# Spectral mixing and S4D convolution on one core: the inverse's first step joined to the kernel taps in two quarters, the products of both halves in one instruction, other planning constants

## The chip, the cores and the metric

One core of one Trainium2 chip. The metric is the device time of one execution in microseconds (us). The kernel before the change takes 584.09 us (median of three runs, 583.81 to 584.11).

## What is computed

Two independent blocks share one program, and their outputs are concatenated. All data are float32.

```
# A: Fourier mixing, x is 2048 x 512
a = einsum("bsd,ed->bse", x, dft_hid_re);  b = einsum("bsd,ed->bse", x, dft_hid_im)
yA = einsum("ts,bse->bte", dft_seq_re, a) - einsum("ts,bse->bte", dft_seq_im, b)
# B: S4D, u is 2048 x 512, state size 128
K  = 2 * real(einsum("dn,dnl->dl", C * dt, exp(A * dt * l)))     # taps, 512 x 2048
yB = irfft(rfft(u, 4096) * rfft(K, 4096), 4096)[:2048] + u * D_skip
```

## The kernel before, in words

**The stream (A).** Both matrix products of A run as one long sequence of 128x128x512 matmuls, 1920 of them (line 366, `acc`). Each operand is split into a rounded part `hi` (ScalarE, line 221) and the rest `lo` (VectorE, line 225), and three matmuls make one product: hi·hi, lo·hi, hi·lo. A call of three is a *stream step*; there are 640. Raw operands arrive in tiles `raw` (7 of them, `RAWS`), are split into pairs of tiles (4 pairs, `DEPTH`); 28 operands go another way, with two GpSimd DMAs (lines 315 and 320).

**The convolution (B)** needs, in order: tables of powers on VectorE (products at line 605, sums at line 614; 16 chunks of 32 channels); for each chunk the *taps*, 64 small matmuls of tables (line 801, in the trace 128 matmuls and as many weight loads, since a float32 matmul appears twice); after two chunks the first DFT step of the taps (line 832); the same for u (line 890); then for each quarter of the channels (h = 0 to 3) and each of four blocks q a *product*: the second DFT step on TensorE (line 992), two ScalarE copies of its two halves out of PSUM (line 1006), on VectorE for each half the two elementwise multiplications (lines 1009 and 1011), then one subtraction (line 1019) and one addition (line 1022); then the *inverse's first step*, 16 small matmuls (line 1029, `f<-uk,ia`), whose result goes to DRAM; and when a quarter's four blocks are there, the *inverse's second step*, two calls of 16 matmuls (line 1078, `f<-zl,ib`).

**What sets the order.** Every engine works in program order, and that order comes from a planner in the kernel (class `Plan`): each piece of work is a generator that asks for an engine with a planned duration and an urgency; the planner always takes the request with the earliest planned start, in grains of `GRAIN` us, and among equals the lowest urgency number. The stream has urgency 5, so it fills TensorE wherever nothing else is ready; a call of another kind is put between stream steps at the moment when the planner thinks its data are there. Going from the stream to other matmuls and back has a planned price. `fetched` models the loading of the instructions. `LATE[h]` is the urgency of quarter h's product. A `Joined` piece can run its matmuls inside the next taps call instead of alone: the mechanism is there before the change, but with `JOIN = 0` no quarter uses it. The buffers `uk` and `z` exist once for quarters 0 to 2 (`b.n` is 1) and twice for quarter 3, so one product must have done its inverse's first step before the next may begin.

Of the kernel before, what the change touches and what calls it, by code (L numbers as in the profile page):

```python
# [11 lines left out]
AF = mybir.ActivationFunctionType  # L12
# [38 lines left out]
STREAM = 5  # L51
GRAIN = 0.05
BLOCK, ASKS, LASTS = 256, 110, 400
ASKED, APART_BY, COMES = 2.0, 3.8, 2.4
APART = None, True
LATE = 1, 1, 3, 1


def HELD():
    return 1  # L60


# [20 lines left out]
class Plan:  # L83
# [111 lines left out]
class Fnet:  # L195
# [149 lines left out]
    def matmuls(self):  # L345
        nc = self.nc
        for g in self.groups:
            still = (self.x, self.x_ev) if g[0] == "s" else (self.w, self.w_ev)
            items, acc = self.items[g], []
            for batch in [[i] for i in items[:-BATCH]] + [items[-BATCH:]]:  # L350
                for d in range(4):
# [3 lines left out]
                    for i in batch:  # L355
# [53 lines left out]
class Joined(Event):  # L409
# [5 lines left out]

    def run(self, got, shared=True):
        self.got, self.users = got, {k: 1 for k, _ in got}
        if shared:
            self.users[got[0][0]] = 2
        self.fn(got)  # L420

# [6 lines left out]
class Ssm:  # L428


    def __init__(self, tc, ctx, plan, fnet, nd, ldt, dsk, uG, f1u, f1k, w2, ia, ib, out):
# [14 lines left out]
        self.t1s, self.t2s, self.css = Sem(2), Sem(1), Sem(2)  # L446
        self.kss, self.res, self.xks = Sem(1), Sem(1), Sem(1)
        self.waiting, self.taps_left, self.pars = [], 16, Sem(1)
        self.sets, self.set_ev = {}, [Event(), Event()]
# [27 lines left out]
    def banks(self, n):  # L477
# [7 lines left out]
        self.plan.put(self.one)  # L485
        return got

    def give(self, k):
# [294 lines left out]
    def taps(self, ks, n, done):  # L783
# [4 lines left out]
        other = self.waiting.pop(0) if self.waiting else None  # L788
        got = yield from self.banks(2 if other else 1)
        k, p = got[0]  # L790
        yield "pe", 1.97 + (1.05 if other else 0), None, 320 if other else 256
        if other:
            other.run(got)
        t1, t2 = self.t1.pop(n), self.t2
# [13 lines left out]
        while self.waiting and not self.taps_left:  # L808
# [3 lines left out]
                             p[:, :, 256:].rearrange("p o (i l) -> p l o i", i=4), AF.Copy)  # L812
        if other:
            other.leave(k)
        else:
            self.give(k)
        done()

    def stage1_k(self, ks, n, ev):
# [6 lines left out]
        got = yield from self.banks(2)  # L826
        yield "pe", 1.11, None, 64
        for a in range(2):
# [50 lines left out]
    def stage1_u(self, k):  # L879
# [4 lines left out]
        got = yield from self.banks(2)  # L884
        yield "pe", 1.13, None, 32
        for r in range(2):
# [94 lines left out]
    def product(self, b, h, q, got, done):  # L981
# [22 lines left out]
        def half(r, k, p):  # L1004
            yield "act", act(1024), HELD
            a.activation(uk[:, r].rearrange("p g c n d -> p g (c n d)"), p, AF.Copy)  # L1006
            self.give(k)
            yield "dve", dve(512)
            v.tensor_tensor(P[:, r], t[:, r], u[:, r], op=OP.mult)  # L1009
            yield "dve", dve(512), *APART  # L1010
            v.tensor_tensor(t[:, r], t[:, r], u[:, r, :, ::-1], op=OP.mult)  # L1011
# [7 lines left out]
        v.tensor_tensor(u[:, :, :, 0], P[:, :, :, 0], P[:, :, :, 1], op=OP.subtract)  # L1019
# [3 lines left out]

        def run(got):
            for c, Y in enumerate((u, t)):
# [6 lines left out]
        if self.taps_left and h < JOIN:  # L1032
            self.waiting.append(w)
            yield w
        if w.got is None:
            got = yield from self.banks(2)
            yield "pe", 1.05, None, 64
            w.run(got, False)
        self.plan.put(b.uks)
# [27 lines left out]
    def inverse(self, b, h, i, n):  # L1067
# [4 lines left out]
        for o in range(0, n, 8):  # L1072
            nc.sync.dma_start(z[:, o:o + 8], self.zs[h].rearrange("s c l d -> (s c) l d")[:, n * i + o:n * i + o + 8])
        (k, ps), = yield from self.banks(1)
        yield "pe", 0.14 + 0.11 * n, None, 4 * n
        for w in range(n // 2):
            for y in range(2):
                nc.tensor.matmul(ps[64 * y:64 * y + 64, w // 4, PART * (w % 4):PART * (w % 4) + PART],  # L1078
                                 self.ib[:, n * i + 2 * w + y], z[:, 2 * w + y], start=True, stop=True,
                                 tile_position=(0, 64 * y))  # L1080
        o = n * i // 2
        for w in range(0, n // 2, 4):
            yield "act", act(512)
            nc.scalar.activation(z[:, w:w + 4], ps[:, w // 4].rearrange("p (w d) -> p w d", w=4), AF.Copy)
        self.give(k)
        yield "dma", load(32 * n, 270)
# [81 lines left out]
```

## Time and profile before

| what | value |
|---|---|
| median of three runs | 584.09 us |
| the profiled execution: its own time | 582.56 us |
| its span, first to last instruction | 580.8 us |
| TensorE busy | 571.1 us, 98% |
| VectorE busy | 512.5 us, 88% |
| ScalarE busy | 371.2 us, 64% |
| GpSimd busy | 40.3 us, 7% |
| granted TensorE clock, mean | 0.999 |

In the page, "PE" is TensorE's matmuls, "PEld" its weight loads, DVE VectorE, ACT ScalarE, POOL GpSimd. A matmul's row lasts longer than the distance to the next one, because matmuls overlap; a VectorE row overlaps the next one a little too. So distances from start to start are what add up, not durations. The span is divided into 40 slices of 14.5 us, with the busy share of each in tenths.

### The profile page before, as it was taken

What the parts mean: (1) busy time and instruction counts of PE and PEld (TensorE: products, weight loads), DVE (VectorE), ACT (ScalarE), POOL (GpSimd) and SP (SyncE); (2) the same over time, 40 slices, a digit from 0 to 9 for tenths busy, and PEclk for the clock granted to TensorE, in tenths of its full rate; (3) what the DMA queues carried; (4) which work ended last, traced back from release to release, by engine and by line L of the source; (5) the groups of instructions that cost most, each with busy time, mean ns of one, the idle gap of its engine ahead of it and who ended that gap; (6) DMA issues with size and microseconds to landing.
All of it is one profiled execution on the core that took longest, in us unless ns stands there. A gap on an engine that the chain in (4) does not pass through costs nothing.

```text
span 580.8 us, 15376 instructions
## 1 busy us (share of the span) xinstructions
PE 571.1 (98%) x6150; PEld 436.1 (75%) x6150; DVE 512.5 (88%) x911; ACT 371.2 (64%) x729; POOL 40.3 (7%) x60
## 2 busy tenths in 40 slices
PE   8999999999999999999999999999999999999996
PEld 6877777788777777778877777777687777776685
DVE  6999999999999999999999999999989999346410
ACT  4779665763777595768568585945588744445522
POOL 0000000000100000100000001001100000000000
PEclk9999999999999999999999999999999999999999
DMA  8999999986469767876797887479989995789564
GB/s 248 327 372 263 280 294 276 285 262 170 133 159 239 207 171 218 205 180 207 207 222 190 237 216 226 125 186 296 243 280 262 243 282 184 209 251 303 169 195 144
DMA packets 147831, 133.10 MB, mean 229 GB/s; under 512 B 47280, under 2 KB 107312, under 8 KB 147504
## 3 DMA queue, kind: packets, MB, share of 16 engines
q1 hardware_dynamic: 139408, 117.05, 66.7%
q0 software_dynamic: 8064, 14.68, 12.6%
q8 instruction: 48, 0.79, 0.6%
q10 hardware_dynamic: 288, 0.39, 0.2%
q14 instruction: 23, 0.19, 0.1%
HBM read 89.36 MB, written 42.73 MB: 227 GB/s over the span
## 4 chain that ended last, share of the span: by engine, by line
PE 70%; DVE 23%; issue 4%; DMA 2%; SPq 0%; ACT 0%; DVEq 0%; ACTq 0%
PE acc L366 55%; DVE prod L605 8%; DVE t L614 4%; PE f L992 4%; PE f L801 3%; DVE lo L225 3%; PE f L1029 3%; PE f L1078 2%; PE f L890 2%; DVE t L634 1%; PE f L832 1%; DVE z L1009 1%; DVE cs L675 1%; DMA zl<-zs 1%; DVE uk L1011 1%
## 5 line engine op out<-in xcount | busy, mean ns | idle before, releaser
L366 PE MATMUL acc<-hi,x_hi 128*128 128x512 f32 x640 | 258.2, 403 | 0.3 <-ACT hi L221 0.3
L366 PE MATMUL acc<-lo,x_hi 128*128 128x512 f32 x640 | 250.2, 391 | 0.0
L366 PE MATMUL acc<-hi,x_lo 128*128 128x512 f32 x640 | 249.7, 390 | 0.1
L605 DVE TENSOR_TENSOR prod<-t,cs 128x1024 f32<-128x1024 f32 (+4 forms) x192 | 163.1, 867 | 1.7 <-ACT t L723 0.6
L366 PEld LDWEIGHTS acc<-hi,x_hi 128*128 128x128 f32 x640 | 120.1, 188 | 49.8 <-issue 23.7
L366 PEld LDWEIGHTS acc<-hi,x_lo 128*128 128x128 f32 x640 | 120.3, 188 | 26.5 <-DVE x_lo L225 0.5
L366 PEld LDWEIGHTS acc<-lo,x_hi 128*128 128x128 f32 x640 | 120.3, 188 | 23.0 <-DVE lo L225 0.2
L221 ACT ACTIVATE hi<-raw 128x512 fp32r<-128x512 f32 x132 | 82.6, 627 | 64.0 <-PE acc L366 48.5
L225 DVE TENSOR_TENSOR lo<-raw,hi 128x512 fp32r<-128x512 f32 x132 | 90.1, 684 | 28.2 <-ACT hi L221 21.9
L614 DVE TENSOR_TENSOR t<-prod 128x512 f32<-128x512 f32 (+4 forms) x192 | 94.0, 511 | 1.0
L621 ACT ACTIVATE square<-t 128x256 f32<-128x256 f32 (+1 forms) x64 | 36.7, 573 | 31.0 <-DVE t L614 28.3
L320 POOL DMA_DIRECT2D lo<-in_sT x28 | 24.3, 868 | 214.1 <-ACT lo L318 33.8
L1006 ACT ACTIVATE uk<-f 128x1024 f32<-128x1024 f32 x32 | 31.1, 1017 | 11.8 <-PE f L992 11.8
L801 PEld LDWEIGHTS f<-t,t 128*32 128x32 f32 x2048 | 29.5, 110 | 7.9 <-issue 5.8
L801 PE MATMUL f<-t,t 128*32 128x64 f32 x2048 | 32.4, 220 | 1.9 <-issue 1.4
L389 ACT ACTIVATE y<-acc 128x512 f32<-128x512 f32 x47 | 28.0, 595 | 8.7 <-PE acc L366 8.6
L1009 DVE TENSOR_TENSOR z<-uk 128x512 f32<-128x512 f32 x32 | 21.9, 684 | 9.6 <-ACT uk L1006 7.4
L315 POOL DMA_DIRECT2D hi<-in_sT x28 | 16.2, 577 | 189.4 <-PE acc L366 147.0
L1044 ACT ACTIVATE z<-f 128x512 f32<-128x512 f32 x32 | 17.7, 592 | 13.3 <-PE f L1029 13.3
L634 DVE TENSOR_TENSOR t<-square 128x128 f32<-128x128 f32 (+1 forms) x64 | 24.6, 385 | 0.0
L992 PE MATMUL f<-xt,w 64*32 64x256 f32 x768 | 23.5, 379 | 0.0
L1011 DVE TENSOR_TENSOR uk<-uk 128x512 f32<-128x512 f32 x32 | 22.1, 690 | 0.9
(94 smaller groups left out, 490.7 us busy)
## 6 DMA issues: line engine op xcount, KB each, us to landing
raw<-in_sT SPq DMA_DIRECT2D x99, 256.0 KB, 5.4
p<-y SPq DMA_DIRECT2D x32, 256.0 KB, 3.2
xk<-xk_sb SPq DMA_DIRECT2D x32, 256.0 KB, 5.2
zs<-z SPq DMA_DIRECT2D x32, 256.0 KB, 3.3
zl<-zs SPq DMA_DIRECT2D x16, 512.0 KB, 5.0
raw<-p SPq DMA_DIRECT2D x32, 256.0 KB, 4.4
hi<-in_sT POOLq DMA_DIRECT2D x28, 256.0 KB, 4.6
lo<-in_sT POOLq DMA_DIRECT2D x28, 256.0 KB, 4.9
```

Of the source, the lines that this page charges most:

```text
L221: self.nc.scalar.activation(hi, src, AF.Copy)
L225: self.nc.vector.tensor_tensor(lo, src, hi.bitcast(F32), op=OP.subtract)
L366: nc.tensor.matmul(acc[d], l[:, cols], r, start=k == 0 and n == 0, stop=k == len(items) - 1 and n == 2)
L389: self.nc.scalar.activation(y, ps, AF.Copy, scale=-1.0 if g[2] == 1 else 1.0)
L605: self.nc.vector.tensor_tensor(p.rearrange("p k d c m -> p k (d c) m"), src.rearrange("p d c l -> p (d c) l")[:, None, :, rows].to_broadca ...
L614: self.nc.vector.tensor_tensor(dst[:, :, :, rows], p[:, 0], p[:, 1, :, ::-1], op=OP.add)
L621: self.nc.scalar.activation(sq, t[:, :, :, m // 2:m], AF.Square)
L634: self.nc.vector.tensor_tensor(t[:, :, 0, m:2 * m:2], box[0][:, :, 0], box[0][:, :, 1], op=OP.subtract)
L801: nc.tensor.matmul(ps[32 * j:32 * j + 32, i], t1[:, d, c], t2[:, d, c], start=c == 0, stop=c == 1, tile_position=(0, 32 * j))
L992: nc.tensor.matmul(got[r][1][32 * xx:32 * xx + 32, g, 256 * c:256 * c + 256], self.w2[rows, 2 * q + r, xx, 32 * c:32 * c + 32], xt[rows].r ...
L1006: a.activation(uk[:, r].rearrange("p g c n d -> p g (c n d)"), p, AF.Copy)
L1011: v.tensor_tensor(t[:, r], t[:, r], u[:, r, :, ::-1], op=OP.mult)
```

## The change

1. `JOIN` 0 becomes 2: in quarters 0 and 1 the inverse's first step waits for the next taps call, and its matmuls run at that call's start, in the same PSUM tiles (columns 0 to 255; the taps use 256 to 511).
2. For quarters 0 to 2 the two multiplications are done for both halves at once, on 128x1024 elements, after both halves have been copied; quarter 3 keeps them by halves.
3. `RAWS` 7 becomes 5, `DEPTH` 4 becomes 5: a raw tile is one 128x512 tile, a split pair is two, so the memory is the same.
4. Planning constants: `GRAIN`, `LATE`, the durations of five kinds of call, and the price of leaving and re-entering the stream (0.11 and 0.09 become 0.14 and 0.11 us). They reach the chip only through the order.
5. Code by which the inverse's second step could be joined as well, with `WAITS = 0`: no quarter uses it.

```diff
-GRAIN = 0.05
+GRAIN = 0.03
-LATE = 1, 1, 3, 1
+LATE = 1, 1, 1.5, 1
...
                 if stream != self.streaming:
-                    dur += 0.11 if stream else 0.09
+                    dur += 0.14 if stream else 0.11
...
-                        yield "pe", 0.683, None, 6
+                        yield "pe", 0.681, None, 6
...
     def taps(self, ks, n, done):
...
         other = self.waiting.pop(0) if self.waiting else None
-        got = yield from self.banks(2 if other else 1)
+        late = self.late.pop(0) if self.late and not other else None
+        got = yield from self.banks(2 if other or late else 1)
         k, p = got[0]
-        yield "pe", 1.97 + (1.05 if other else 0), None, 320 if other else 256
+        users = {k: 1}
+        yield "pe", 1.97 + (1.05 if other else IB if late else 0), None, 320 if other or late else 256
...
     def product(self, b, h, q, got, done):
...
             self.give(k)
-            yield "dve", dve(512)
-            v.tensor_tensor(P[:, r], t[:, r], u[:, r], op=OP.mult)
-            yield "dve", dve(512), *APART
-            v.tensor_tensor(t[:, r], t[:, r], u[:, r, :, ::-1], op=OP.mult)
+            if h == 3:
+                yield from times(slice(r, r + 1), LAST)
             left[0] -= 1
             if not left[0]:
                 self.plan.set(ready)
+
+        def times(r, urgency=None):
+            n = 512 * (r.stop - r.start)
+            yield "dve", dve(n), urgency
+            v.tensor_tensor(P[:, r], t[:, r], u[:, r], op=OP.mult)
+            yield "dve", dve(n), urgency, True
+            v.tensor_tensor(t[:, r], t[:, r], u[:, r, :, ::-1], op=OP.mult)
         for r in range(2):
             self.plan.spawn(half(r, *got[r]), LATE[h])
         yield ready
+        if h < 3:
+            yield from times(slice(0, 2))
...
-            yield "pe", 1.05, None, 64
-            w.run(got, False)
+            yield "pe", 1.15 + (IB if late else 0), None, 128 if late else 64
...
-CHUNK, FIRST, JOIN = 32, 128, 0
-RAWS, DEPTH, STAGED, AHEAD = 7, 4, 4, 3
+CHUNK, FIRST, JOIN = 32, 128, 2
+RAWS, DEPTH, STAGED, AHEAD = 5, 5, 4, 3
+WAITS = 0
+IB = 0.14 + 0.11 * 16
```

The planned duration of the other three kinds of call changes in the same way: the taps' first DFT step 1.11 to 1.06, u's first step 1.13 to 1.25, the inverse's first step alone 1.05 to 1.15.

**Where the rows stand now: TensorE, the last block of quarter 0, before and after.** Line 366 (370 after) is the stream, 1029 (1050) the inverse's first step, 801 (816) the taps. Before, the inverse's first step stands alone between stream matmuls:

```order
L366 MATMUL acc<-hi,x_lo_323 128x512
L1029 MATMUL f_3274<-uk,ia 64x256 x2
L1029 MATMUL f_3275<-uk,ia 64x256 x2
L1029 MATMUL f_3274<-uk,ia 64x256 x2
L1029 MATMUL f_3275<-uk,ia 64x256 x2
L1029 MATMUL f_3274<-uk,ia 64x256 x2
L1029 MATMUL f_3275<-uk,ia 64x256 x2
L1029 MATMUL f_3274<-uk,ia 64x256 x2
L1029 MATMUL f_3275<-uk,ia 64x256 x2
L366 MATMUL acc<-hi,x_hi_349 128x512
```

After:

```order
L370 MATMUL acc<-hi,x_lo_247 128x512
L1050 MATMUL f_3732<-uk,ia 64x256 x2
L1050 MATMUL f_3733<-uk,ia 64x256 x2
L1050 MATMUL f_3732<-uk,ia 64x256 x2
L1050 MATMUL f_3733<-uk,ia 64x256 x2
L1050 MATMUL f_3732<-uk,ia 64x256 x2
L1050 MATMUL f_3733<-uk,ia 64x256 x2
L1050 MATMUL f_3732<-uk,ia 64x256 x2
L1050 MATMUL f_3733<-uk,ia 64x256 x2
L816 MATMUL f_3732<-t_124,t_3161 32x64 x64
L370 MATMUL acc<-hi,x_hi_246 128x512
```

The taps now follow the inverse's first step without a stream matmul between; this is so eight times. Counted over the whole TensorE order, the stream is cut into 72 runs before and into 65 after (one taps call that stood beside an inverse's second step before stands alone after). The eight joined calls come after 254, 285, 313, 347, 371, 411, 439 and 471 of the 640 stream steps; before, the same eight stood alone after 230, 251, 274, 296, 366, 388, 406 and 427. From the last taps call on (551 stream steps before it in both orders) the same calls follow in both, in a slightly different order, and the last inverse's second steps stand after 633 and 635 steps in both.

**VectorE, the first product of quarter 0.** Lines 1009 and 1011 (1031 and 1033 after) are the multiplications, 1019 and 1022 (1040 and 1043) the subtraction and the addition, 605 and 614 (615 and 624) table work, 225 the split. Before:

```order
L614 TENSOR_TENSOR t_2096<-prod 128x64x8
L675 TENSOR_TENSOR cs<-seed 128x704
L1009 TENSOR_TENSOR z<-uk 128x512
L1011 TENSOR_TENSOR uk<-uk 128x4x128
L1009 TENSOR_TENSOR z<-uk 128x512
L1011 TENSOR_TENSOR uk<-uk 128x4x128
L605 TENSOR_TENSOR prod<-t_2096,cs 128x1024
L1019 TENSOR_TENSOR uk<-z 128x4x128
L225 TENSOR_TENSOR lo<-raw,hi 128x512
L1022 TENSOR_TENSOR uk<-uk 128x4x128
```

After:

```order
L624 TENSOR_TENSOR t_2100<-prod 128x32x16
L615 TENSOR_TENSOR prod<-t_2100,cs 128x1024
L1031 TENSOR_TENSOR z<-uk 128x1024
L1033 TENSOR_TENSOR uk<-uk 128x8x128
L624 TENSOR_TENSOR t_2100<-prod 128x32x16
L1040 TENSOR_TENSOR uk<-z 128x4x128
L1043 TENSOR_TENSOR uk<-uk 128x4x128
```

Four multiplications have become two of twice the size, in each of twelve products.

More of the change, by code (lines that the diff above doesn't have):

```diff
@@ L55, with LAST @@
 APART = None, True
-LATE = 1, 1, 3, 1
+LATE = 1, 1, 1.5, 1
 def HELD():
     return 1
+def LAST():
+    return LATE[3]
 def FAST():
@@ L486, in banks, with ia_done @@
         return got
+    def ia_done(self):
+        self.ia_left -= 1
+        while len(self.late) > self.ia_left:
+            self.plan.set(self.late.pop(0))
     def give(self, k):
@@ L1073, in inverse, with run @@
             nc.sync.dma_start(z[:, o:o + 8], self.zs[h].rearrange("s c l d -> (s c) l d")[:, n * i + o:n * i + o + 8])
[L1074 to L1080, printed above, removed]
[L1081 to L1085 removed]
+        o = n * i // 2
+        def run(got, zone):
+            for w in range(n // 2):
+                for y in range(2):
+                    if len(got) == 2:
+                        to = got[w // 4][1][64 * y:64 * y + 64, w // 2 % 2, zone + PART * (w % 2):zone + PART * (w % 2 + 1)]
+                    else:
+                        to = got[0][1][64 * y:64 * y + 64, w // 4, PART * (w % 4):PART * (w % 4) + PART]
+                    nc.tensor.matmul(to, self.ib[:, n * i + 2 * w + y], z[:, 2 * w + y], start=True, stop=True,
+                                     tile_position=(0, 64 * y))
+        j = Joined(self, run)
+        if h < WAITS and self.ia_left > len(self.late):
+            self.late.append(j)
+            yield j
+        if j.got is None:
+            got = yield from self.banks(1)
+            yield "pe", IB, None, 64
+            j.run(got, {})
+        for m in range(2):
+            yield "act", act(512)
+            to = z[:, 4 * m:4 * m + 4]
+            if len(j.got) == 2:
+                src = j.got[m][1][:, :, j.zone:j.zone + 2 * PART].rearrange("p b (w d) -> p b w d", w=2)
+                to = to.rearrange("p (b w) d -> p b w d", b=2)
+            else:
+                src = j.got[0][1][:, m].rearrange("p (w d) -> p w d", w=4)
+            nc.scalar.activation(to, src, AF.Copy)
+            if len(j.got) == 2:
+                j.leave(j.got[m][0])
+        if len(j.got) == 1:
+            j.leave(j.got[0][0])
         yield "dma", load(32 * n, 270)
```

34 lines of the change are left out of this document (22 added, 12 removed).

## Prediction, made before the changed kernel was run

> **What bounds the kernel now.** I read the page's busy times and slices first, then stretches of 50 us, then the groups of TensorE's instructions, then the timeline where TensorE leaves the stream.
>
> ```profile
> span 580.8 us, 15376 instructions
> PE 571.1 (98%) x6150; PEld 436.1 (75%) x6150; DVE 512.5 (88%) x911; ACT 371.2 (64%) x729; POOL 40.3 (7%) x60
> ...
> PE   8999999999999999999999999999999999999996
> ...
> DVE  6999999999999999999999999999989999346410
> ```
>
> ```profile
> 100.00:150.00 50.00, 50.00 (x486) 40.75 (x485) 49.66 (x89) 29.23 (x63) 6.16 (x9) 1.00 0.82 230
> 200.00:250.00 50.00, 49.83 (x591) 37.59 (x593) 49.45 (x85) 37.25 (x71) 4.84 (x7) 1.00 0.78 209
> 350.00:400.00 50.00, 50.00 (x614) 38.94 (x603) 49.65 (x90) 31.32 (x64) 5.71 (x8) 1.00 0.68 185
> 500.00:550.00 50.00, 50.00 (x564) 36.69 (x564) 25.40 (x39) 25.61 (x40) 0.00 (x0) 1.00 0.81 240
> ```
>
> The columns after the stretch are its length and the busy time of PE, PEld, DVE, ACT and POOL. TensorE is full to the end, and until about 490 us VectorE is as full (49.45 to 49.66 of 50 us). So two engines bound the first five sixths at once, TensorE alone the rest. A gain needs less time on TensorE, and what VectorE makes for it must come earlier by as much.
>
> ```profile
> L366 PE MATMUL acc<-hi,x_hi 128*128 128x512 f32 x640 | 258.2, 403 | 0.3 <-ACT hi L221 0.3
> L366 PE MATMUL acc<-lo,x_hi 128*128 128x512 f32 x640 | 250.2, 391 | 0.0
> L801 PE MATMUL f<-t,t 128*32 128x64 f32 x2048 | 32.4, 220 | 1.9 <-issue 1.4 <-DVE t L614 0.4
> L1029 PE MATMUL f<-uk,ia 32*64 32x256 f32 x512 | 20.2, 389 | 0.3
> ```
>
> The last columns are busy time, mean ns, and the idle time ahead. The stream hardly ever waits (0.3 us), so it isn't short of operands. What TensorE can lose is at the changes between stream and small calls, and in pauses inside these.
>
> **Term 1, the cuts.** One taps call that already stands beside another small call, and one that stands alone:
>
> ```profile
> 429.32 0.39 PE L366 MATMUL acc<-lo,x_hi 128*128 128x512 f32 x1
> 429.55 0.39 PE L366 MATMUL acc<-hi,x_lo 128*128 128x512 f32 x1
> 429.87 1.99 PE L801 MATMUL f<-t,t 128*32 128x64 f32 x128
> 431.79 1.97 PE L1078 MATMUL f<-zl,ib 128*64 128x128 f32 x32
> 433.69 0.50 PE L366 MATMUL acc<-hi,x_hi 128*128 128x512 f32 x1
> 434.02 0.39 PE L366 MATMUL acc<-lo,x_hi 128*128 128x512 f32 x1
> ```
>
> ```profile
> 488.09 0.39 PE L366 MATMUL acc<-hi,x_lo 128*128 128x512 f32 x1
> 488.41 1.99 PE L801 MATMUL f<-t,t 128*32 128x64 f32 x128
> 490.33 0.50 PE L366 MATMUL acc<-hi,x_hi 128*128 128x512 f32 x1
> 490.67 0.40 PE L366 MATMUL acc<-lo,x_hi 128*128 128x512 f32 x1
> ```
>
> Starts in the stream are 0.23 us apart (429.32 to 429.55). Leaving it takes 0.32 (429.55 to 429.87), 0.09 too much; the first step back takes 0.33 to 0.34, 0.11 too much. Between taps and next call there is nothing extra: 429.87 to 431.79 is 1.92, as is the lone call to the stream. So each cut costs 0.20. The order has 72 stream runs before and 65 after, seven cuts fewer: 7 × 0.20 = **1.4 us** off TensorE.
>
> **Term 2, pauses in the inverse's first step.** A clean one and two others:
>
> ```profile
> 435.95 1.12 PE L1029 MATMUL f<-uk,ia 32*64 32x256 f32 x32
> ```
>
> ```profile
> 232.65 1.77 PE L1029 MATMUL f<-uk,ia 32*64 32x256 f32 x32
> ```
>
> ```profile
> 314.94 1.36 PE L1029 MATMUL f<-uk,ia 32*64 32x256 f32 x32
> ```
>
> ```profile
> 314.88 0.68 DVE L1022 TENSOR_TENSOR uk<-uk 128x512 f32<-128x512 f32 x1
> ```
>
> At 314.94 the call begins while VectorE's last addition (line 1022) still runs, to 315.56; its second half needs that sum. It was put where the plan expected the data, with no reserve. Sixteen clean calls would be 16 × 1.12 = 17.9; the group row has 20.2 busy and 0.3 idle, so 2.6 us are pauses. Both pauses shown lie in quarters 0 and 1, the calls that the change joins; the clean call is one of quarter 2. In a taps call the data are long there, since the call waits for tables: 2.6 us go. But quarter 2's four calls stay alone, and its urgency goes from 3 to 1.5, near the 1 that quarters 0 and 1 have. What they then lose lies between nothing (as now) and 2.6 / 8 = 0.33 each; nearer is the latter, so 4 × 0.33 = 1.3 come back. Net **1.3 us**.
>
> **Term 3, VectorE's share.** The first product of quarter 0:
>
> ```profile
> 186.77 0.68 DVE L1009 TENSOR_TENSOR z<-uk 128x512 f32<-128x512 f32 x1
> 187.49 0.69 DVE L1011 TENSOR_TENSOR uk<-uk 128x512 f32<-128x512 f32 x1
> 188.10 0.68 DVE L1009 TENSOR_TENSOR z<-uk 128x512 f32<-128x512 f32 x1
> 188.81 0.69 DVE L1011 TENSOR_TENSOR uk<-uk 128x512 f32<-128x512 f32 x1
> 189.42 1.22 DVE L605 TENSOR_TENSOR prod<-t,cs 128x1024 f32<-128x1024 f32 x1
> 190.56 0.68 DVE L1019 TENSOR_TENSOR uk<-z 128x512 f32<-128x512 f32 x1
> ```
>
> Four multiplications take 186.77 to 189.42, 2.65 us: 0.72 from the first of a pair to the second, which overwrites what the first read, and 0.61 from there on. A 128x1024 product takes 1.14 from start to start, so the merged pair takes 1.14 + 0.12 + 1.14 = 2.40: 0.25 saved per product, 12 × 0.25 = **3.0 us**. On VectorE this is path while the tables last:
>
> ```profile
> 487.48 0.68 DVE L614 TENSOR_TENSOR t<-prod 128x512 f32<-128x512 f32 x1
> ```
>
> This sum ends at 488.16, and the last taps start at 488.41: VectorE leads by a quarter of a microsecond (about 1 us counted to the half of the call that reads this sum). After the last taps both orders have the same TensorE work. So the end can come earlier only by what the last taps do: the lesser of TensorE's saving, 1.4 + 1.3 = 2.7, and VectorE's, 3.0 and some lead. **2.7 us.**
>
> What the merging may cost: it must wait for both copies.
>
> ```profile
> 183.12 1.94 ACT L1006 ACTIVATE uk<-f 128x1024 f32<-128x1024 f32 x2 [0.74 <-PE f L992]
> ```
>
> Both were done at 185.06, 1.7 us before the first multiplication started; table work stood between, and in the new order it does too. I take 0; the other end is a whole second copy, 1.94 / 2 = 0.97 us of idle VectorE, in all twelve (11.6 us). Behind the waiting multiplication stand splits and table work, and for these the stream and the taps wait.
>
> [...]
>
> **Edits at nothing.** Five raw tiles and five pairs: the stream waits 0.3 us in all, so there is nothing to win in it. A raw tile is in use from issue to split.
>
> ```profile
> raw<-in_sT SPq DMA_DIRECT2D x99, 256.0 KB, 5.4
> ```
>
> The transfer lands 5.4 us after its issue (the last column, a median), and five operands of the stream are at least 20 stream steps of 0.68, 13.6 us. If that cover fails, the stream stops for hi or lo; I allow 1 us each way, by the 0.3 us it has now. The plan's prices and grain act through the order alone, which is counted above. The later stores of quarters 0 and 1 are hidden: their second steps come long before the end, and the last second steps stand where they stood (after 633 and 635 of 640 steps).
>
> **The rivals.** *Instruction supply* (ends on the other side):
>
> ```profile
> 405.56 1.88 PE L801 MATMUL f<-t,t 128*32 128x64 f32 x118
> 408.86 0.41 PE L801 MATMUL f<-t,t 128*32 128x64 f32 x10 [1.43 <-issue]
> ```
>
> ```profile
> q8 instruction: 48, 0.79, 0.6%
> ```
>
> One taps call stops for 1.43 us on nothing that the profile shows. 12300 matmuls and weight loads over 48 instruction transfers are 256 each; ahead of this call the order has a product (128 instructions) and only nine stream matmuls, then 256 of taps. I take it for late instructions. A joined call holds 320, more than a transfer, in 3.0 us. For it: a product follows several joined calls after nine stream matmuls. Against it: the other fifteen taps calls show no such stop, and the order puts stream between. I leave one stop in, as now. Each further one costs 1.43; from two on (2.9 against 2.7) the gain is gone, four give 5.7 - 2.7 = 3.0 lost: 587.1 us.
>
> [...]
>
> *Waits take the place of the gain*: TensorE, ahead by 2.7, waits at taps, k steps and quarter 2 for a VectorE that isn't faster, because new order costs it the 3.0. For it: VectorE leads the last taps by a quarter us only. Then 0 to 1 us remain: 583.6.
>
> *The merged wait*: VectorE idles for the second copy in six of twelve products: 5.8 - 3.0 = 2.8 lost, 586.9; it decides from three on (2.9). Against it the 1.7 us above.
>
> *More*: no pause in quarter 2 and no stop for instructions: 2.7 + 1.3 + 1.4 = 5.4 saved, if VectorE's lead and a shorter idle allow it: 578.7. That the change doesn't do what it says is excluded by the order: the eight calls are joined.
>
> **How the numbers follow.** The profiled execution took 582.56 us, its span 580.8 with 1.8 around it; the sum gives 579.9 for it. The median of the runs is 1.5 higher than that execution; all do the same work, so I take 2.7 from 584.09: **581.4 us**, by itself 579.9 to 582.9. Chances: forecast 0.53, more 0.14, waits 0.18, instruction supply 0.10, merged wait 0.05. About 0.2% (1.2 us) is what a measurement of this kernel can tell from no change. Faster: 0.53 + 0.14 = 0.67; same: 0.18; slower: 0.15. The range, 578.6 to 585.2, takes in *more* down to its centre, the forecast, *waits* and the 1 us for the tiles; it leaves out the two slower rivals and the tail of *more*.
>
> **What would show it.** Right: joined calls of about 3.05 us from first matmul to the stream, no pause in them; line 1031 at 1.22 us, starting after the copies without idle time; 65 cuts; the last taps near 485.5 us. Wrong: idle time of VectorE before line 1031 released by line 1020; more rows with an "issue" stop; pauses in taps released by line 624; stream steps waiting for lo.

## The result, and the profile after

The changed kernel takes **589.61 us** (median of six runs, 587.23 to 592.76); the kernel before, run beside it, 583.9 us (582.23 to 584.11, six runs). The ratio is 1.0102, with a 95% interval of 1.0069 to 1.0135: about 6 us slower, where 2.7 us faster was predicted. The profiled execution is the slowest of the six (592.76 us, span 591.0). A second profiled execution of the same kernel, called *again* below, took 585.40 us (span 583.6). The two differ by more than the change is worth, so I read both. In one later run an execution of the kernel before took 1127.61 us; it is left out everywhere.

The page of the changed kernel, first profile: busy times, and the slices of TensorE and VectorE.

```profile
span 591.0 us, 15330 instructions
PE 574.1 (97%) x6150; PEld 439.3 (74%) x6150; DVE 511.4 (87%) x887; ACT 368.8 (62%) x729; POOL 40.2 (7%) x60
...
PE   8999999999999999999999999999989997999996
...
DVE  6999999999999999999999699999999996463510
```

VectorE has 24 instructions fewer, as it should. But there is a dent in its row that was not there before: the digit 6 in the 23rd slice, 325 to 340 us. TensorE has a slight one in the 30th slice (428 to 443 us) and a deeper one in the 34th (488 to 502). The stretches show the places at 325 and 488 us again, first in the kernel before, then in the changed one (columns: start and end, length, then busy time of PE, PEld, DVE, ACT, POOL, then the granted clock, DMA share and GB/s):

```profile
300.00:350.00 50.00, 49.93 (x617) 37.04 (x617) 49.38 (x91) 36.55 (x71) 4.28 (x6) 1.00 0.81 211
450.00:500.00 50.00, 50.00 (x647) 38.52 (x647) 45.41 (x76) 27.37 (x51) 0.00 (x0) 1.00 0.80 230
```

```profile
300.00:350.00 50.00, 49.20 (x545) 38.58 (x530) 45.02 (x79) 31.10 (x65) 5.80 (x9) 1.00 0.86 239
350.00:400.00 50.00, 49.94 (x647) 38.36 (x646) 49.71 (x86) 38.80 (x81) 4.17 (x6) 1.00 0.70 185
450.00:500.00 50.00, 45.81 (x613) 33.77 (x615) 45.78 (x74) 24.27 (x46) 0.00 (x0) 0.93 0.87 251
```

From 350 to 400 us VectorE is full. From 300 to 350 us it lacks 4.4 us of what it had before, and from 450 to 500 us TensorE lacks 4.2. The groups of TensorE:

```profile
L370 PE MATMUL acc<-hi,x_hi 128*128 128x512 f32 x640 | 259.2, 405 | 6.2 <-ACT y L393 5.0 <-ACT x_hi L225 1.1
L816 PE MATMUL f<-t,t 128*32 128x64 f32 x2048 | 31.9, 220 | 0.8 <-DVE zl L918 0.5 <-ACT uk L1020 0.3
L1050 PE MATMUL f<-uk,ia 32*64 32x256 f32 x512 | 18.5, 387 | 0.1
L1110 PE MATMUL f<-zl,ib 128*64 128x128 f32 x256 | 16.0, 276 | 2.4 <-DMA zl<-zs 1.6 <-ACT lo L322 0.8
```

The inverse's first step is down from 20.2 to 18.5 us: most of its pauses have gone (sixteen clean calls would be 17.9). In their place the stream, which waited 0.3 us before, waits 6.2, and the inverse's second step 2.4. A joined call, in TensorE's timeline:

```profile
210.36 1.12 PE L1050 MATMUL f<-uk,ia 32*64 32x256 f32 x32
211.41 1.99 PE L816 MATMUL f<-t,t 128*32 128x64 f32 x128
```

The inverse's part takes 1.05 us to the first matmul of the taps, and the next stream matmul starts at 213.33: 2.97 us from the first matmul to the stream, without a pause. All eight take as long.

**Where VectorE stops.** Who VectorE waited for from 10 to 496 us (total, times, longest), in the kernel before:

```profile
DVE x_lo L225 <- ACT x_hi L221: 1.2, 1, 1.2
DVE prod L605 <- ACT t L723: 0.6, 1, 0.6
DVE lo L225 <- ACT hi L221: 0.3, 1, 0.3
DVE seed L654 <- ACT seed L652: 0.2, 1, 0.2
```

And in the changed kernel, first profile:

```profile
DVE lo L229 <- ACT hi L225: 5.2, 2, 3.6
DVE cs L685 <- ACT seed L676: 2.2, 1, 2.2
DVE prod L615 <- ACT t L733: 1.3, 1, 1.3
DVE prod L615 <- ACT t L753: 0.7, 1, 0.7
DVE zl L916 <- ACT zl L914: 0.7, 1, 0.7
DVE seed L664 <- ACT seed L662: 0.2, 1, 0.2
```

2.3 us became 10.3 (6.0 in *again*). The largest part that all profiles of this order share is this, in VectorE's timeline:

```profile
329.23 0.89 DVE L685 TENSOR_TENSOR cs<-seed 128x704 f32<-128x704 f32 x1 [2.17 <-ACT seed L676]
331.70 1.29 DVE L229 TENSOR_TENSOR lo<-raw,hi 128x512 fp32r<-128x512 f32 x2 [1.57 <-ACT hi L225]
333.72 0.85 DVE L615 TENSOR_TENSOR prod<-t,cs 128x128 f32<-128x128 f32 x2 [0.73 <-ACT t L753]
```

2.17 + 1.57 + 0.73 = 4.5 us. VectorE waits for ScalarE's seeds of chunk 11 (the sines and exponentials from which a chunk's tables start), then for a split's rounded part that stands behind them, then for a copied piece of the tables. ScalarE's timeline in the same profile:

```profile
315.40 0.63 ACT L631 ACTIVATE square<-t 128x512 f32<-128x512 f32 x1 [2.79 <-DVE t L644]
...
316.89 0.26 ACT L658 ACTIVATE seed<-par 128x64 f32<-128x64 f32 x1
...
322.49 0.50 ACT L668 ACTIVATE seed<-seed 128x352 f32<-128x352 f32 x1 [3.48 <-DVE seed L666]
...
323.50 1.28 ACT L670 ACT_TABLE_LOAD   x1
...
326.35 1.28 ACT L672 ACT_TABLE_LOAD   x1
...
328.62 0.58 ACT L676 ACTIVATE seed<-seed,halfpi 128x352 f32<-128x352 f32 x1
```

The two engines wait for each other in turn: ScalarE 2.79 us for a table instruction (line 644) and 3.48 us for VectorE's part of the seeds, and then VectorE 4.5 us for what is left of ScalarE's chain, which has two table loads of 1.28 us in it. ScalarE, 62% busy, is idle in the one half and is waited for in the other. In the kernel before, the same product of seeds started right behind VectorE's previous instruction:

```profile
318.75 0.89 DVE L675 TENSOR_TENSOR cs<-seed 128x704 f32<-128x704 f32 x1
```

**Where the stream stops.** TensorE's timeline in the first profile:

```profile
488.71 0.39 PE L370 MATMUL acc<-hi,x_lo 128*128 128x512 f32 x1
493.20 0.79 PE L370 MATMUL acc<-hi,x_hi 128*128 128x512 f32 x1 [4.10 <-ACT y L393]
493.79 0.63 PE L370 MATMUL acc<-lo,x_hi 128*128 128x512 f32 x1
...
498.57 1.99 PE L816 MATMUL f<-t,t 128*32 128x64 f32 x128
```

The accumulators are evicted by ScalarE; its timeline, and that of SP's queue:

```profile
491.00 0.63 ACT L225 ACTIVATE hi<-raw 128x512 fp32r<-128x512 f32 x1 [5.86 <-DMA raw<-p]
```

```profile
470.44 1.52 SPq L979 DMA_DIRECT2D xt<-xu  x2
...
484.68 0.47 SPq L979 DMA_DIRECT2D x_lo<-xu  x1
485.25 0.41 SPq L401 DMA_DIRECT2D out_ya<-y  x1
485.76 1.35 SPq L338 DMA_DIRECT2D raw<-p  x3
```

ScalarE stands for 5.86 us at a copy of a raw tile, and the evictions stand behind it. The tile's load was issued at 485.76 us, behind 15 us of spectrum loads (line 979). In *again* the same stop is 1.40 us.

**The account.** Up to the last table sum (line 614, after: 624) I add up all gaps between the end of one VectorE instruction and the start of the next; what is left of the time (with 0.8 us ahead of the first instruction) is VectorE's work. Behind the sum come the last taps and what follows them. In microseconds, for one profiled execution of each kernel (some of the others are told below):

| execution | VectorE's work | its gaps | last sum at | from there to the end | span |
|---|---|---|---|---|---|
| before | 477.4 | 10.7 | 488.2 | 92.6 | 580.8 |
| again | 476.2 | 14.5 | 490.7 | 92.9 | 583.6 |
| first profile of the change | 476.2 | 19.7 | 496.0 | 95.0 | 591.0 |
| raw7 | 476.1 | 15.9 | 492.0 | 94.9 | 586.9 |
| burst_pool | 476.2 | 16.4 | 492.6 | 93.5 | 586.1 |
| rawp_pool | 476.0 | 14.2 | 490.2 | 96.2 | 586.4 |
| halves | 477.2 | 18.7 | 495.9 | 96.3 | 592.2 |
| par_act | 476.2 | 16.8 | 493.0 | 93.8 | 586.8 |
| noexp11 | 476.1 | 14.3 | 490.5 | 94.4 | 584.8 |
| noexp11_raw | 476.1 | 12.5 | 488.6 | 94.2 | 582.9 |
| before_noexp11 | 477.4 | 10.5 | 487.9 | 92.4 | 580.3 |
| before_idle | 477.8 | 16.6 | 494.3 | 92.7 | 587.0 |

So the change saves VectorE 1.2 us of work, and its order costs VectorE 3.8 us of gaps in *again* and 9 in the first profile. The account is bookkeeping: it says where VectorE's time went, not yet that a gap lengthens the whole. Where clearly more than 92.6 us remain after the last sum, TensorE itself was late: in the first profile the last taps start at 498.57 us, 2.6 after the sum, because of the stop of 4.10 us and the slow steps behind it.

### The profile page after: what moved, and what is told of

The parts are those of the page before. It is cut to its first block, busy times and chain, and to the rows that moved or that the text cites. A ratio compares the mean times of both kernels' runs of the same rounds, so it can differ in the third digit from the quotient of the medians.

```text
span 591.0 us, 15330 instructions
## 1 busy us (share of the span) xinstructions
PE 574.1 (97%) x6150; PEld 439.3 (74%) x6150; DVE 511.4 (87%) x887; ACT 368.8 (62%) x729; POOL 40.2 (7%) x60
## 4 chain that ended last, share of the span: by engine, by line
DVE 41%; PE 34%; DMA 10%; issue 7%; ACT 5%; SPq 2%; DVEq 0%; ACTq 0%
PE acc L370 27%; DVE prod L615 14%; DVE t L624 8%; DVE lo L229 6%; PE f L1006 2%; DMA xk<-xk_sb 2%; DVE t L644 2%; PE f L1110 2%; PE f L1050 2%; DVE t L638 1%; DVE z L1031 1%; PE f L816 1%; DMA zl<-zs 1%; DMA zs<-z 1%; DMA p<-y 1%
## 5 line engine op out<-in xcount | busy, mean ns | idle before, releaser
L615 DVE TENSOR_TENSOR prod<-t,cs 128x1024 f32<-128x1024 f32 (+3 forms) x192 | 163.5, 870 | 3.3 <-ACT t L733 1.3
L319 POOL DMA_DIRECT2D hi<-in_sT x28 | 16.4, 586 | 227.8 <-PE acc L370 113.1
L1031 DVE TENSOR_TENSOR z<-uk 128x1024 f32<-128x1024 f32 (+1 forms) x20 | 20.1, 1007 | 9.6 <-ACT uk L1020 8.6
L690 ACT ACTIVATE cs<-cs 128x352 f32<-128x352 f32 x32 | 15.8, 533 | 12.0 <-DVE cs L685 11.9
L638 DVE SCALAR_TENSOR_TENSOR t<-t 128x128 f32<-128x128 f32 (+2 forms) x48 | 22.4, 467 | 0.3
(94 smaller groups left out, 491.6 us busy)
```

The source lines that it names most:

```text
L615: self.nc.vector.tensor_tensor(p.rearrange("p k d c m -> p k (d c) m"), src.rearrange("p d c l -> p (d c) l")[:, None, :, rows].to_broadca ...
L638: self.nc.vector.scalar_tensor_tensor(t[:, :, 1, m:2 * m:2], t[:, :, 0, m // 2:m], 2.0, t[:, :, 1, m // 2:m], op0=OP.mult, op1=OP.mult)
```

## The experiments

Two theories stood at the start: the loss lies in **single stops** that one can take away one by one (tiles, burst of loads, size of the multiplications), or in **the order** as a whole. Later the question was which engine carries it.

**again, raw7, burst_pool** keep the changed order to the row.

```diff
 again: nothing
 raw7:       name="raw", bufs=RAWS  ->  bufs=7
 burst_pool: quarter 3's 16 loads of u's spectrum: nc.sync.dma_start -> nc.gpsimd.dma_start
```

> The changed kernel once more, for a second trace and a time on the chip of the next three runs. Theory S (supply): TensorE loses time in a few long stops, because stream operands (raw) and other transfers reach the in-order queue of SyncE late; the one at 488 us in the first trace (4.3 us, and 2.3 us more at a lower granted clock) comes back, since ScalarE waits there for a raw operand whose transfer is queued behind sixteen spectrum loads. Expected 587 to 592 us, with a stop of 3 to 5 us between 485 and 495 us. Rival J (jitter): that stop was an accident of one execution; then it is missing here, and the 3 to 8 us over the kernel before are spread over many small waits.

> The changed kernel with its order of instructions on every engine kept to the row, but seven raw tiles in memory instead of five. Theory S1: SyncE's queue stands at raw loads until a split has freed one of five tiles (87 us of such waits in the trace after, 38 before), and everything behind it is late; with seven tiles these waits fall below 40 us and the time falls to 583 to 585 us. Rival S2 (order): the stop comes from where the order puts the raw loads, behind sixteen spectrum loads that SyncE issues one after the other without waiting for tiles; then two more tiles change little, 587 to 590 us, and the stop at about 488 us stays.

> The changed kernel with quarter 3's sixteen loads of u's spectrum issued from GpSimd's queue, which has nothing else to do there; the order on TensorE, VectorE and ScalarE is kept to the row. Rival S2: the raw loads behind them on SyncE are issued some 10 us earlier, the stop at about 488 us (4.3 us and 2.3 us of lower clock) disappears, 583 to 586 us. Theory S1: the tiles are still five, so the raw loads wait for splits instead, and at most half of it goes: 586 to 589 us. Rival J: no change, 587 to 592 us.

Measured, against the kernel before, run beside them: *again* 1.0101 (1.0071 to 1.0131), 588.55 us; raw7 1.0101 (1.0075 to 1.0128), 588.25; burst_pool 1.0086 (1.0065 to 1.0107), 587.88. The stop of 3 to 5 us that was expected in *again* came as one of 1.40. In raw7 the time that SP's queue stood at loads of raw tiles until a split (line 229) freed one fell from 87.3 to 21.2 us, and the time stayed: with this order the number of raw tiles is not the cause. burst_pool took away the stream's stop at 487 us, and 0.7 us of the median, which is within the noise: at an inverse's second step (447.7 us) TensorE waited 3.1 us for its data from DRAM instead.

**only_tiles, only_join, undo_join, grain** let the planner make another order.

```diff
 only_tiles (kernel before): RAWS, DEPTH = 7, 4  ->  5, 5
 only_join  (kernel before): JOIN = 0  ->  2
 undo_join  (changed kernel): JOIN = 2  ->  0
 grain      (kernel before): GRAIN = 0.05  ->  0.03
```

> The kernel before with five raw tiles and five split pairs instead of seven and four, nothing else (the planner makes a new order from it). Theory S1: the shorter reach of the loads alone costs time, 586 to 590 us against 584. Rival S2: it costs something only if the new order puts loads late; 583 to 586 us, and no stop over 2 us in the stream. The inverse's last second step now stands at the very end of the order, which may add up to 3 us by itself.

> The kernel before with the inverse's first step joined to the taps in quarters 0 and 1 and nothing else changed (the planner makes a new order, with 60 stream runs instead of 72, and its last two calls stand behind the stream's end, which adds 4 to 6 us by itself). Theory P (the join is the guilty part: it holds both pairs of PSUM banks, so products wait for their copies): stops of products of 2 us or more in sum, as in the changed kernel (2.6 us), and all stops together over 13 us. Rival R (no part is guilty; any new order has calls that come too early on the chip, since the plan leaves no reserve): the stops stand in other places, and products' stops are under 1 us. Time by P 588 to 592, by R 584 to 595 us.

> The changed kernel with the join taken back (JOIN = 0), all else as changed; the planner makes a new order with 69 stream runs and an early end (last second steps after 619 of 640 stream steps). Theory P: the products' stops go, 580 to 583 us. Rival R: stops of 10 us or more in other places, 584 to 592 us.

> The kernel before with the planner's grain 0.03 instead of 0.05 us and nothing else: no work is added or taken away, only the order is another one (70 stream runs instead of 72; the last call stands behind the stream, which adds 2 to 4 us by itself). Rival R: stops rise from 9 us to 12 or more, 586 to 594 us in all. Theory P: stops stay at 9 to 10 us, 583 to 587 us with the end.

Measured: only_tiles 610.06 us, 1.0467 (1.0436 to 1.0499); only_join 601.49, 1.031 (1.0264 to 1.0355); undo_join 594.58, 1.0192 (1.0141 to 1.0243); grain 585.43, 1.003 (1.0012 to 1.0049). grain leaves every engine the same work (6150 matmuls, 911 VectorE and 729 ScalarE instructions), changes only the order, and is slower than the kernel before. Only its time lies in a range that was expected; only_tiles and only_join lie far above theirs. Taking the joined calls back doesn't take the loss away, it adds to it. Each new order has its own stops; in only_join, for example, they sit at the very end, where the last second step waits for its data from DRAM:

```profile
587.25 6.59 PE L1078 MATMUL f<-zl,ib 128*64 128x128 f32 x64 [8.54 <-DMA zl<-zs]
```

The loss of these orders is not in VectorE's gaps ahead of the last sum. In only_join, only_tiles and grain the last sum ends at 484.1, 485.5 and 487.0 us, earlier than the 488.2 of before, and 115.4, 123.3 and 96.9 us follow it instead of 92.6 (other calls stand there, too). The parts therefore don't add up, and "one part alone" doesn't measure that part here.

**halves, rawp_pool** keep the changed order again.

```diff
 halves: each merged multiplication as two of 128x512, at the same place
 rawp_pool: the 32 loads of raw from p: nc.sync.dma_start -> nc.gpsimd.dma_start
```

> The changed kernel with its order kept, but each merged multiplication written as two on 512 columns at the same place, after both copies, as the merged one: this prices the merging by itself. If VectorE paces TensorE until the last taps, as the prediction has it, 12 pairs at 0.14 to 0.25 us make it 2 to 3 us slower than the changed kernel, 590 to 592 us. If stops elsewhere set the time, it is the same within 1 us, 587.5 to 589.5 us.

> The changed kernel with the stream's 32 loads of its second phase (raw from p) issued from GpSimd's queue instead of SyncE's; the order on TensorE, VectorE and ScalarE is kept. Theory S2: the stop at 487 us comes from these loads standing behind sixteen spectrum loads on SyncE; on their own queue they start as soon as a tile is free, the stop and the lower clock behind it go, and, unlike when the spectrum loads were moved, no transfer is brought forward that delays the inverse's second step: 583 to 586 us. Rival R: the next tight place takes over, 586 to 589 us.

Measured: halves 590.4 us, 1.0119 (1.0053 to 1.0186), not to be told from *again*; in the account its VectorE has 1.0 us more work (477.2 against 476.2). That is what the merging by itself is worth to VectorE. rawp_pool 587.88, 1.0096 (1.0072 to 1.0119): the stop at 487 us is gone, one of 2.3 us at a first DFT step of the taps (493.6 us, for VectorE's line 838) came, and the time is within the noise of *again*.

**lat38, lat48, before_lat48** give the planner a later landing of the DMAs than 3.3 us, in case its reserves are too small.

```diff
-HOP, RESULT, LATENCY = 0.3, 0.15, 3.3
+HOP, RESULT, LATENCY = 0.3, 0.15, 3.8    (lat38; 4.8 in lat48, and in before_lat48 on the kernel before)
```

> The changed kernel with 3.8 instead of 3.3 us in the plan for a transfer's landing; the planner makes a new order with about the same end (last second steps after 632 and 635 stream steps, 65 stream runs). Theory R with the transfers as what is planned too tightly: stops that end with a transfer or stand behind SyncE's queue fall below 4 us in sum, 582 to 586 us. If the reserve of ScalarE's copies is what lacks, they stay: 586 to 590 us.

> The same with 4.8 us, near the landings that the traces show (4.5 to 5.8 us); the new order ends its last second steps after 611 and 613 of 640 stream steps, so nothing stands near the end. Theory R: fewest stops of all the orders with the join, under 9 us in sum, 579 to 583 us, faster than the kernel before or equal. If ScalarE's copies lack the reserve: 584 to 588 us.

> The kernel before with 4.8 instead of 3.3 us for a transfer's landing in the plan and nothing else (73 stream runs, last second steps after 612 and 614). Theory R: 580 to 584 us, stops at or below the 9 us of before. If it is slower than the changed kernel with the same constant by about 2 us, the join's saved cuts show up once the stops are alike; if it is equal or faster, the join gains nothing even with reserve.

Measured: lat38 588.6 us, 1.0106 (1.0081 to 1.013); lat48 611.59, 1.0501 (1.0465 to 1.0538); before_lat48 618.9, 1.063 (1.0604 to 1.0657). More planned reserve doesn't help; the last two lie 24 and 35 us above the ranges that were expected. In lat48 TensorE's longest waits from 200 us on are not for DMAs but for tables and "issue" (nothing that the profile shows):

```profile
PE f L1006 <- issue: 4.2, 2, 2.5
PE f L816 <- issue: 3.6, 2, 3.3
PE f L816 <- DVE t L624: 3.4, 2, 2.6
```

**noexp11, before_noexp11, before_idle, par_act.** By now one thing was common to all profiles of the changed order: VectorE's 4.5 us at 328 to 334 us. Theory V: VectorE sets the pace up to the last taps, so this stop goes into the time; the rival: it is made good later. noexp11 leaves out the exponential of chunk 11 and puts a scaled copy in its place; in its trace ScalarE has no table load from 315 to 336 us, where the first profile has two of 1.28 us.

```diff
 noexp11, before_noexp11 (after's order and before's):
-        a.activation(e, e, AF.Exp, scale=-1.0)
+        a.activation(e, e, AF.Copy if ck == 11 else AF.Exp, scale=-2.0 ** -12 if ck == 11 else -1.0)
 before_idle (before's order):
-        a.activation(k, r, AF.Abs)
+        for _ in range(11 if ck == 11 else 1):
+            a.activation(k, r, AF.Abs)
 par_act (after's order): self.nc.sync.dma_start(self.par[ck], ...) -> self.nc.scalar.dma_start(...)
```

> The changed kernel, its order kept to the row; only chunk 11's exponential on ScalarE is replaced by a scaled copy, which takes the chunk's two ACT_TABLE_LOADs of 1.28 us out of ScalarE's chain (this part of the seeds is left out of the computation). Theory V, that VectorE sets the pace up to the last taps, and loses 4.5 us at 328 to 334 us because it waits there for ScalarE's seeds of chunk 11 (stops of 2.17, 1.57 and 0.75 us before lines 685, 229 and 615): the three stops shrink from 4.5 to 2 us or less, and the time falls by 2.2 to 4.5 us, to 584 to 586.5. The rival, that these stops are made good later because TensorE's own waits decide: within 0.7 us of the changed kernel, 587.5 to 589.5.

> The kernel before with the same edit, as the control: VectorE has no stop over 0.25 us there between 10 and 412 us, and reaches chunk 11's product of seeds 1.4 us after ScalarE's last seed. Theory V and its rival both: within 0.5 us of the kernel before.

> The kernel before, its order kept; ScalarE takes the absolute value of chunk 11's seeds eleven times instead of once (the result is the same), some 4.3 us more before the seeds are done, 1.4 of which VectorE's lead covers. Theory V: VectorE stops for about 3 us near 320 us, and the time rises by 2 to 3.5 us. The rival, that such a stop is made good by the end: less than 1 us more.

> The changed kernel, its order kept; the loads of a chunk's parameters are issued from ScalarE's queue instead of SP's, where chunk 11's stands behind five transfers and is issued at 310.1 us instead of 299.6. Theory V as far as the late load is its cause: seeds begin earlier than 315.7 us, the stops of VectorE at 328 us shrink, and the time falls by 2 to 4.5 us. Theory V with ScalarE's order as the cause (the seeds stand behind a square that waits for VectorE until 314.2 us, whatever the load does): the stops stay, and the time is within 0.7 us of the changed kernel.

before_idle shows the largest effect of the four: 588.87 us, 1.0103 (1.009 to 1.0116), **6.1 us slower** than the kernel before. The ten extra instructions are 5.3 us of ScalarE (5.80 for eleven against 0.50 for one). VectorE's waits from 10 to 496 us:

```profile
DVE lo L225 <- ACT hi L221: 5.0, 2, 4.4
DVE prod L605 <- ACT t L724: 1.2, 2, 0.6
DVE x_lo L225 <- ACT x_hi L221: 1.2, 1, 1.2
DVE ks L825 <- ACT ks L812: 0.5, 1, 0.5
```

7.9 us instead of 2.3, and in the account 16.6 us of gaps instead of 10.7: 5.9 us more of gaps, 6.1 of time. The expectation had only 2 to 3.5 us, since it looked at the product of seeds and not at the split (line 225) that stands ahead of it on VectorE and behind the seeds on ScalarE; and the delay left three small stops further on. TensorE shows the other end of the chain, a second half of an inverse's first step:

```profile
320.49 1.16 PE L1030 MATMUL f<-uk,ia 32*64 32x256 f32 x16 [4.53 <-DVE uk L1023]
```

Behind this stop the stream's matmuls start 0.42 to 0.43 us apart instead of 0.23:

```profile
322.18 0.63 PE L366 MATMUL acc<-lo,x_hi 128*128 128x512 f32 x1
322.60 0.63 PE L366 MATMUL acc<-hi,x_lo 128*128 128x512 f32 x1
```

Row by row against the kernel before, whose order is the same, the stream is set back by 7.1 us here; 1.2 of this come back up to 426 us, most of it at the stop of 1.43 us, which is 0.39 here. VectorE's table sums are set back by 6.5 us, and 0.7 of this come back. So both full engines end 5.8 to 5.9 us late. The run shows that a delay of ScalarE, handed on by VectorE to TensorE, reaches the end almost in full. It doesn't show which of the two carried it there.

The control, before_noexp11, is 582.37 us, 0.9994 (0.9985 to 1.0002): the shorter chain of ScalarE brings nothing where VectorE doesn't wait for it. noexp11 is 586.38 us, 1.0066 (1.0047 to 1.0085), 2.2 us under *again* (another chip), though the intervals overlap. Its VectorE still stops there:

```profile
326.34 0.89 DVE L685 TENSOR_TENSOR cs<-seed 128x704 f32<-128x704 f32 x1 [0.77 <-ACT seed L676]
328.98 1.29 DVE L229 TENSOR_TENSOR lo<-raw,hi 128x512 fp32r<-128x512 f32 x2 [1.75 <-ACT hi L225]
331.03 0.87 DVE L615 TENSOR_TENSOR prod<-t,cs 128x128 f32<-128x128 f32 x2 [0.76 <-ACT t L753]
```

3.3 us instead of 4.5, though 2.6 us of table loads are gone: ScalarE then waited 1.13 us for an accumulator to evict. Row by row against *again*, whose order is the same, noexp11's table sums start 0.1 us earlier at 303 us and 1.5 us earlier at 414, 452 and 481 us. The stream's steps follow: 0.1 us earlier at 281 us, 1.15 at 346, 1.5 at 469 and 485. So what VectorE gained at this place stayed for 150 us, as V has it. Then a late raw tile takes 1.3 us of it from VectorE, and a stop of 2.60 us with slow steps behind it (1.40 without them in *again*) puts the stream 1.2 us late, so that the profiled execution is the longer one (584.8 against 583.6). In the time as a whole noexp11 agrees with V only in sign.

par_act is 588.23 us, 1.0091 (1.007 to 1.0112), the same as *again*. It doesn't settle what it was made for: ScalarE's queue issued chunk 11's load at 311.42 us, no earlier than SP's did (311.29). That the load isn't the cause is read from ScalarE's rows above: line 658 follows the copies ahead of it without idle time, and what ScalarE waited for before them was a table instruction of VectorE (line 644).

**noexp11_raw** takes away what noexp11 still loses at 486 us.

```diff
 noexp11 with the edits of raw7 and rawp_pool
```

> noexp11 (the changed kernel's order, chunk 11's exponential left out) with the two edits of raw7 and rawp_pool besides: seven raw tiles in memory, and the 32 loads of raw from p on GpSimd's queue. What VectorE loses at 485 to 490 us in noexp11 (2.15 us, for ScalarE's copy of a late raw tile) should shrink to under 1 us. If stops of VectorE add up to the time, this one is 0.7 to 2 us under noexp11, at 584.4 to 585.7; if the late transfers don't matter once VectorE is behind, it is within 0.5 us of noexp11.

Measured: 586.38 us (584.68 to 588.48), 1.0067 (1.0042 to 1.0092), the median of noexp11. Its profiled execution was the fastest of the six, with gaps of 12.5 us and a span of 582.9. The stop at 486 us is gone, the median isn't lower, as the second of the two expectations had it; what decides the other executions isn't shown by this one profile. No version with the changed order beat the kernel before.

## Why the prediction was wrong

**Term 1, the cuts: right.** The stream has 65 runs, and a cut has the price it had: in the median 0.32 us out of the stream and 0.34 for the first step back, before as after. So the seven cuts save the 1.4 us that were predicted; waits have taken their place.

**Term 2, the pauses: right in quarters 0 and 1**, see the joined call above, 2.97 us to the stream for about 3.05. In quarter 2 one call has a pause, 1.25 us in *again* (released by line 860 on VectorE) and 0.72 in the first profile. I had taken 1.3 us in four small pauses, so that this size came out is partly luck.

**Term 3, VectorE's share: mis-sized.** I took 12 × 0.25 = 3.0 us from the first product of quarter 0. From start to start, less idle time, each of the eleven products before the last sum spends 2.55 us on multiplications before and 2.34 in *again*: 11 × 0.21 = 2.3 us. Of this, 1.1 went again in the new neighbourhoods: the table products alone (192 instructions) take 153.5 us instead of 153.1, for the same work. Net 1.2 us.

**The sum: this is the step that failed.** "The lesser of TensorE's saving and VectorE's" assumes that VectorE goes on without stops in the new order. I had shown that it was full (49.45 to 49.66 of 50 us), and that it led the last taps by a quarter of a microsecond, so I had reason to expect that a stop of VectorE would go into the time. But I counted the planning constants and the new order as "act through the order alone, which is counted above", and had counted only TensorE's cuts and VectorE's durations, no wait. The sum that the traces give for *again* against before is -1.2 (work) + 3.8 (gaps) + 0.3 (behind the last sum) = 2.9, with spans of 583.6 and 580.8. The last taps, forecast near 485.5 us, start at 490.9. That time VectorE gains or loses in this order stays is shown by noexp11's rows, 1.5 us over 150 us; that a delay handed on through VectorE reaches the end, by before_idle, in which TensorE was set back as far.

*again* is the fastest execution of the changed kernel; the medians differ by about 6 us. Row by row, the first profile falls 7.4 us behind *again* at three places: 1.2 at the start, where a tile of x comes late, 1.4 between 420 and 470 us, at an inverse's second step that waits for its data, and 4.8 at the raw tile at 487 us and the slow steps behind it. All three begin with a wait for a transfer, which the sum of the prediction had at nothing as well. For the executions without a profile this is not shown.

**The rivals.** *Waits take the place of the gain* was the nearest, but half right in its mechanism: waits did take the gain and more, yet TensorE waits little for VectorE in *again* (0.5 us at taps, 0.3 at a k step, 0.6 in quarter 2, and 1.6 at the start as before). Its longest waits are for ScalarE's evictions, 2.3 us, and VectorE's are for ScalarE, too. I bounded this rival by the 3.0 us that the change was to save, though nothing bounds an order's waits by that. *Instruction supply* didn't come: the first profile shows no "issue" stop among TensorE's waits, *again* one of 0.30 us, and the 1.43 us one of before is gone. That the 48 transfers of row q8 carry TensorE's instructions, 256 each, was my estimate; no row names their engine. The joined calls, 320 each, took 2.97 us. *More* didn't come either: that stop went, but a pause in quarter 2 came, and the new waits took up the rest. *The merged wait*: up to the last sum, line 1031 isn't among the lines of VectorE's waits in the first profile (shown above); its waits for ScalarE's copies, 8.6 us at four instructions, all lie behind the last sum, where VectorE is busy for 36.0 of 95.0 us. The five raw tiles cost nothing that could be measured (raw7).

Two things stay open: why the planner puts chunk 11's seeds where the engines wait for each other, since its own times for this place were not compared with the chip's; and why transfers come late in some executions of the changed kernel, which differ by 7 us (585.40 to 592.76 over all runs), where those of the kernel before stay within 5 (581.38 to 586.28).

## What to carry to other kernels

When two engines are full at once, an edit's saving can be the smaller part of the forecast (here 1.2 us of VectorE's work against 3.8 us of new gaps in *again*): before taking it, go through the busier producer's rows in the new order and ask at each wait on another engine how far ahead that engine stands, since what is lost there can stay lost to the end (in before_idle 5.8 to 5.9 us of 6.5 to 7.1). Where a planner makes the order, any change of a constant is a new draw: a change of `GRAIN` alone, with the same work on every engine, cost 0.3%, and single parts of this change 3 to 5%. To see whether a delay is made good, add one on purpose and see whether the time grows by as much; then look in the rows which engines it set back, for in before_idle it was two.

## What was not expected of the hardware

After some stops the stream runs at half speed. Around the stop in the first profile (the granted clock is the third number from the end):

```profile
493.20:498.50 5.30, 5.30 (x12) 3.80 (x12) 5.27 (x8) 3.33 (x5) 0.00 (x0) 0.50 0.97 340
498.50:504.00 5.50, 5.50 (x171) 4.23 (x171) 3.14 (x6) 1.32 (x3) 0.00 (x0) 1.00 0.27 74
```

At a granted clock of 0.50, twelve stream matmuls start 0.43 us apart instead of 0.23: the stop of 4.10 us costs about 2.4 more. In the clock record of this execution the stretch at 0.50 lasts 6.83 us, from 491.6 to 498.5 us, so it begins within the stop. The length of the stop alone doesn't decide: stops of 1.93 us (raw7) and 2.60 us (noexp11) had such a tail, with stream matmuls 0.43 us apart from 490.7 and 489.5 us on; stops of 1.40 us (*again*, 0.23 us apart behind it) and 2.57 us (par_act, a granted clock of 1.00 from 480 to 500 us) had none. What does decide isn't shown here.
